# A two-network block on one core: the second network in three tiles of 1024 tokens instead of four of 768

## The chip, the core and the metric

The kernel runs on one core of one Trainium2 chip. The core has five engines with instruction streams of their own: TensorE (PE) multiplies matrices, VectorE (DVE) and ScalarE (ACT) do element-wise work, GpSimd (POOL) does slower element-wise work, SyncE (SP) issues most DMAs. Products are summed in PSUM, eight banks of 512 float32 columns on 128 partitions; everything else lives in SBUF. The metric is the device time of one launch in microseconds; lower is better.

## The reference

`x` holds 4096 tokens of 640 numbers in float32. A modulation vector scales two networks that are added to `x` one after the other. The first mixes in the frequency domain (Fourier transform along the tokens, small complex layers, inverse transform). The second is a gated feed-forward network:

```python
x = A_x
mod = (_silu(c) @ w_mod).reshape(c.shape[0], 6, 1, -1)
sa, ca, ga, sb, cb, gb = (mod[:, 0], mod[:, 1], mod[:, 2], mod[:, 3], mod[:, 4], mod[:, 5])
h = _layernorm(x, axis=-1) * (1 + ca) + sa
x = x + ga * _A_ref(h, A_w1, A_b1, A_w2, A_b2)
h = _layernorm(x, axis=-1) * (1 + cb) + sb
x = x + gb * ((_silu(h @ w_gate) * (h @ w_up)) @ w_down)
```

`w_gate` and `w_up` are 640 x 1728, `w_down` is 1728 x 640.

## The kernel before

The first network takes the first 307 us and isn't touched, apart from the last rows of it: the inverse transform of most row blocks is done while the second network runs. A *row block* is 128 tokens, and there are 32.

**Products in three parts.** Float32 products are made from a high and a low part of each operand: high by high, high by low, low by high, three products on PE. So each weight and each activation is *split*: ACT writes the high part, DVE subtracts it to get the low part.

**Tiles.** `TL` (L1142) lists the tiles of the second network as (first row block, half the number of row blocks H). Tiles 0 and 1 (`NS` = 2) have 4 row blocks, 512 tokens, and are computed plainly (`plain`, L1983). Tiles 2 to 5 have 6 row blocks, 768 tokens, in two halves of H = 3. Each of their weight pairs is a *unit of seven* (`seven`, L2104): a 2 x 2 block product by Winograd's form of Strassen's scheme, 7 block products instead of 8, with 128 H = 384 columns each, and then the fifth slice of the 640 inputs (`fifth`). In order: B11, T3, B21, fifth, T2, T4, fifth, T1, B22, fifth, fifth. A block product is 6 products on PE, a fifth 3.

**Stages of a tile.** `WG` lists 14 weight pairs: g and u (gate and up, 256 columns of the hidden 1728) for p = 0 to 5, s (the last 64 columns of both, stage 2, `rest` in tiles 2 on) and m (128 columns of both, last). `STG` orders them: g0, u0, s, g1, down 0, u1, g2, down 1, and so on to u5, m, down 5. A down stage adds the hidden columns of one p to the output of the tile's row blocks, in products of 320 columns; down 5 also adds the tail (hidden 1536 on; weights `NPR`). In tiles of `DT` (L1163: the last two) the down stage is itself a block product with seven parts per pair of row blocks (`down7`, L2265), else it is `down` (L2385).

**Places.** `bufs` (L1182) gives the number of SBUF places for each tag. R and h1: raw gate and up weights. wb: their split form. wt: the block sums T1 to T4 of a unit, in two halves (T3 and T2; T4 and T1), made once from the raw weights by `sum_w` (POOL, ACT, DVE) in tiles 0 and 1, written to DRAM (`td`) and loaded by each later tile (`load_t`, L2517). wd, wdh, wdl: raw down weights, high and low part. h0 to h7: a tile's normalised, split tokens, read back from DRAM (`hsd`) by `load_h` (L1854) in the order `HORD`; the unit uses h0, h6, h1, h3 (fifth), h5, h2, h4, h7 in this order. ho: tokens on their way to DRAM.

**Rows.** For each later tile `row_chain` (L1831) finishes the first network pair by pair of row blocks: load, gate (POOL), split, inverse transform (PE, `py`), residual and layer norm, transposes (PE, `pt`), the sums for seven block products, split, and four stores to `hsd`. `W` in `pair_steps` are these stores.

**Order.** The program order of each engine is made while the kernel is built. `slot` moves a model clock ahead with PE's products; `sweep` lets each chain of steps, in order of priority, issue what its model says is due. `until` forces a step that PE now needs. Places are taken and given back in the model through `room`. On the chip the order is fixed and semaphores hold each instruction until its operands are there; each engine's stream and SP's stream of DMA issues run strictly in order.

Of the kernel before, what the change touches and what calls it, by code (L numbers as in the profile page):

```python
# [6 lines left out]
F32 = mybir.dt.float32  # L7
# [159 lines left out]
def body(tc, x, w1, b1, w2, b2, wg, wu, wd, c, wm, k_fa, k_tb, k_tx, k_bx, k_ga, k_ge, k_id, out, dbg=None):  # L167
# [29 lines left out]
    with ExitStack() as top:  # L197
# [939 lines left out]
        with ExitStack() as ff:  # L1137
# [4 lines left out]
            TL = [(0, 2), (4, 2), (8, 3), (14, 3), (20, 3), (26, 3)]  # L1142
# [8 lines left out]
            NW = len(WG)  # L1151
            STG = []
# [10 lines left out]
            DT = (4, 5)  # L1163
# [18 lines left out]
            bufs = {"R": 2, "h1": 1, "wb": 2, "wt": 3, "wd": 1, "wdh": 2, "wdl": 2, "pc": 4, "px": 2, "gt": 2, "ho": 2,  # L1182
# [183 lines left out]
            place("wt", [P, 2, 2, 2, P], F32R, 2, "wt0_0a")  # L1366
            place("R", [P, 5, 256], F32, 2, "r0_2")
            place("h1", [P, 5, 256], F32, 1, "r0_1")
            ht0 = [fp.tile([P, 2, 512], F32R, tag=f"h{j}", bufs=1, name=f"ht0_{j}") for j in HT0]
            place("h0", [P, 4, 2, P], F32, 1, "ts0")  # L1370
            place("pc", [P, D], F32, 4, "cr0_0")
            place("px", [P, D], F32, 2, "x0_0")
            place("wd", [P, 2, D], F32, 1, "wdr0_0")
# [32 lines left out]
            prep, wld, wtl, down_w, left_l, x2_l, sums, parts, outs = [chain() for _ in range(9)]  # L1406
# [8 lines left out]
            def rtag(t, n):  # L1415
                return "h1" if t < NS and n % 3 == 1 else "R"

            def load_w(t, n):
# [3 lines left out]
                def load():  # L1422
                    r = raw[t, n] = take(tag, [P, 5, 256], F32, bufs[tag], f"r{t}_{n}")
# [7 lines left out]
                return Step("S", 2.1, load, key=("raw", t, n), use=(tag,))  # L1431


            def prep_w(t, n):
# [4 lines left out]

                def high(ks, e=slice(0, c)):  # L1440
                    if (t, n) not in wbs:
                        wbs[t, n] = take("wb", [P, 2, 5, 256], F32R, 2, f"wb{t}_{n}")
                    act.activation(wbs[t, n][:, 0, ks, e], raw[t, n][:, ks, e], AF.Copy)  # L1443

                def low(ks, e=slice(0, c)):
                    (pool if onp else dve).tensor_tensor(wbs[t, n][:, 1, ks, e], raw[t, n][:, ks, e],  # L1446
# [4 lines left out]
                if spl:  # L1451
# [3 lines left out]
                        raw[t, n][:, k2, e2], raw[t, n][:, 1:4:2, 0:P], raw[t, n][:, 0:4:2, 0:P], op=OP.subtract),  # L1455
# [64 lines left out]
            def block_loads(t, p):  # L1520
                def load(hl, s):
                    if s == 0:
                        wds.setdefault((t, p), {})
                    q = ("wdh", "wdl")[hl]
                    w = take(q, [P, 2, D], F32R, 2, f"{q}{t}_{p}_{s}").rearrange("p a (b e) -> p (a b) e", b=2)
                    n = 4 - s
                    nc.sync.dma_start(f32(w[:, 0:n]), wsd[p, :, hl, 4 * s:4 * s + n])
                    for i in range(n):
                        wds[t, p][BL[4 * s + i], hl] = w[:, i]

                if p == NPR:
                    def tail(hl, f):
                        w = wds.setdefault((t, p), {})
                        if hl:
                            w[hl, f] = take("px", [P, D], F32R, 2, f"tl{t}_{f}")
                            nc.sync.dma_start(f32(w[hl, f]), wsd[p, :, 1, 2 * f:2 * f + 2])
                        else:
                            v = take("h32", [P, 2, D], F32R, 1, f"th{t}")
                            nc.sync.dma_start(f32(v.rearrange("p a b -> p (a b)")),
                                              wsd[p, :, 0, 0:4].rearrange("p a b -> p (a b)"))  # L1540
                            w[0, 0], w[0, 1] = v[:, 0], v[:, 1]

                    d = tuple(("wst", p, x) for x in TB) + (("dend", t, 0),)
                    return [Step("S", 1.7 - 0.8 * hl, lambda hl=hl, f=f: tail(hl, f), d, ("wdb", t, p, hl, f),
                                 ("px",) if hl else ("h32",), bulk=0.8) for hl, f in ((0, 0), (1, 0), (1, 1))]

                return [Step("S", 2.1 - 0.4 * s, lambda hl=hl, s=s: load(hl, s),
                             tuple(("wst", p, x) for x in BL), ("wdb", t, p, hl, s), (("wdh", "wdl")[hl],), bulk=(3.0, 0.8, 0.8, 0.8, 0.8, 3.0)[p])
                        for s in range(2) for hl in range(2)]
# [43 lines left out]
            def prep_wd(t, p):  # L1593
# [19 lines left out]

                def high(f):
# [974 lines left out]
```

## Time and profile before

| | us |
|---|---|
| median of 3 runs (1423.55 to 1424.76) | 1424.37 |
| the profiled execution | 1426.34 |
| its span in the profile | 1424.6 |
| first network and start | 0 to 307 |
| tile 0, tile 1 (plain, 4 row blocks) | 307 to 454, 454 to 605 |
| tiles 2 and 3 (units of seven, `down`) | 605 to 821, 821 to 1036 |
| tiles 4 and 5 (units of seven, `down7`) | 1036 to 1228, 1228 to 1425 |

The profile is of one execution. Engines are PE, DVE, ACT, POOL and SP; a *line* is the line of the kernel that issued an instruction. "xN" counts instructions, "idle before, releaser" tells what ended an engine's idle time. PEclk is the granted clock of TensorE, 1.00 being full speed. Matmuls overlap in the pipeline, so that the time of one product is read from the distance of starts over a stretch, not from the duration of one.

### The profile page before, as it was taken

The page shows a single profiled execution, that of the slowest core. Times are in us where ns is not written, and L with a number is a line of the kernel's source. Part 1 is how long each engine was busy: PE and PEld are TensorE (multiplying, and loading weights), DVE is VectorE, ACT ScalarE, POOL GpSimd, SP SyncE. Part 2 cuts the span into 40 slices and gives each one's busy share as a digit, 9 for nine tenths or more (in the row PEclk, how much of TensorE's full clock was granted, in tenths as well). Part 3 has the DMA queues.
Part 4 walks back from the last instruction along what each step waited for, and adds up shares of the span by engine and source line. Part 5 has one row for each costly group of instructions (what it writes and reads, how often), then busy time and mean ns, then how long its engine had stood idle before and what let it go on. Part 6 is the DMA issues. An engine that isn't in the chain of part 4 may idle for free.

```text
span 1424.6 us, 24438 instructions
## 1 busy us (share of the span) xinstructions
PE 1392.1 (98%) x8840; PEld 1309.0 (92%) x8840; DVE 1094.9 (77%) x1983; ACT 732.9 (51%) x1495; POOL 535.2 (38%) x633
## 2 busy tenths in 40 slices
PE   6899999999999999999999999999999999999999
PEld 2699999868888888999999999999999999999998
DVE  8888898798786888578878777888657668567765
ACT  7855555555544654455455456555444345245432
POOL 5300330145453544224334434433325454145532
PEclk9999999999999999999999999999999999999999
DMA  9966677568669979997877998688886667966652
GB/s 376 327 226 207 215 246 240 193 192 262 256 208 341 311 261 301 350 326 237 280 273 256 358 348 279 236 269 280 307 311 232 215 218 239 354 223 215 207 191 85
DMA packets 183178, 372.17 MB, mean 261 GB/s; under 512 B 21360, under 2 KB 104368, under 8 KB 181392
## 3 DMA queue, kind: packets, MB, share of 16 engines
q1 hardware_dynamic: 175200, 355.12, 72.1%
q0 software_dynamic: 6272, 12.85, 2.8%
q10 hardware_dynamic: 1584, 2.62, 0.5%
q8 instruction: 70, 1.15, 0.3%
q14 instruction: 52, 0.43, 0.1%
HBM read 265.68 MB, written 104.86 MB: 260 GB/s over the span
## 4 chain that ended last, share of the span: by engine, by line
PE 64%; DVE 7%; DMA 3%; ACT 2%; issue 1%; POOL 1%; SPq 0%; DVEq 0%; ACTq 0%; POOLq 0%
PE pd L2458 14%; PE pw L2139 8%; PE pw L2141 8%; PE pw L2140 8%; PE pd_X L2320 5%; PE pd_Y L2320 3%; PE pw L2150 2%; PE pw L2152 2%; PE pw L2151 2%; PE pg L2004 2%; PE pg L2003 2%; PE pg L2005 2%; DMA cr<-s 2%; DVE wb L1446 1%; PE pd_Z L2320 1%
## 5 line engine op out<-in xcount | busy, mean ns | idle before, releaser
L2458 PE MATMUL pd<-wdh,a 128*128 128x320 f32 x1040 | 240.1, 311 | 1.3 <-DVE x L2430 1.3
L2458 PEld LDWEIGHTS pd<-wdh,a 128*128 128x128 f32 x1040 | 177.2, 189 | 1.9 <-DVE x L2430 1.6
L2458 PE MATMUL pd<-wdl,a 128*128 128x320 f32 x540 | 166.9, 310 | 0.0
L1446 DVE TENSOR_TENSOR wb<-r,wb 128x512 fp32r<-128x512 f32 (+3 forms) x154 | 154.3, 1012 | 12.2 <-ACT wb L1443 10.3
L2139 PE MATMUL pw<-h,wt 128*128 128x384 f32 x416 | 141.3, 340 | 2.2 <-ACT s_x L2158 2.2
L2141 PE MATMUL pw<-h,wt 128*128 128x384 f32 x416 | 140.4, 337 | 0.0
L2140 PE MATMUL pw<-h,wt 128*128 128x384 f32 x416 | 140.1, 337 | 0.0
L2430 DVE TENSOR_TENSOR x<-x,pd 128x320 f32<-128x320 f32 x240 | 109.8, 479 | 36.9 <-PE pd L2458 32.5
L1443 ACT ACTIVATE wb<-r 128x512 fp32r<-128x512 f32 (+3 forms) x170 | 117.4, 704 | 33.3 <-PE pw L2152 25.7
L2139 PE MATMUL pw<-h,wb 128*128 128x384 f32 x312 | 105.1, 337 | 0.9 <-DVE x L2430 0.9
L2140 PE MATMUL pw<-h,wb 128*128 128x384 f32 x312 | 104.8, 336 | 0.0
L2141 PE MATMUL pw<-h,wb 128*128 128x384 f32 x312 | 104.7, 336 | 0.0
L2005 PE MATMUL pg<-ht,wb 128*128 128x512 f32 x260 | 101.7, 391 | 1.6 <-DVE wb L1446 1.6
L2003 PE MATMUL pg<-ht,wb 128*128 128x512 f32 x260 | 102.4, 394 | 0.0
L2458 PEld LDWEIGHTS pd<-wdl,a 128*128 128x128 f32 x540 | 102.0, 189 | 0.3
L2004 PE MATMUL pg<-ht,wb 128*128 128x512 f32 x260 | 101.6, 391 | 0.0
L2158 ACT ACTIVATE s_x<-pw 128x384 f32<-128x384 f32 x52 | 25.4, 489 | 120.8 <-PE pw L2141 120.0
L2139 PEld LDWEIGHTS pw<-h,wt 128*128 128x128 f32 x416 | 78.2, 188 | 3.5 <-ACT s_x L2158 3.5
L1674 POOL TENSOR_TENSOR cr<-cr,gab 128x640 f32<-128x640 f32 x28 | 47.7, 1707 | 88.6 <-DMA cr<-s 74.0
L2140 PEld LDWEIGHTS pw<-h,wt 128*128 128x128 f32 x416 | 78.2, 188 | 0.0
L2141 PEld LDWEIGHTS pw<-h,wt 128*128 128x128 f32 x416 | 78.1, 188 | 0.0
L2294 DVE TENSOR_TENSOR x<-x,pd_X 128x320 f32<-128x320 f32 x144 | 64.5, 484 | 14.3 <-PE pd_X L2320 14.3
(345 smaller groups left out, 3872.9 us busy)
## 6 DMA issues: line engine op xcount, KB each, us to landing
wt<-td SPq DMA_DIRECT2D x104, 512.0 KB, 5.2
hs<-ho SPq DMA_DIRECT2D x52, 512.0 KB, 5.7
h<-hs SPq DMA_DIRECT2D x32, 768.0 KB, 9.0
r<-in_B_w_up_dram SPq DMA_DIRECT2D x36, 640.0 KB, 5.4
r<-in_B_w_gate_dram SPq DMA_DIRECT2D x36, 640.0 KB, 5.0
wdr<-wdd SPq DMA_DIRECT2D x25, 640.0 KB, 5.4
td<-wt SPq DMA_DIRECT2D x25, 512.0 KB, 5.5
g<-s SPq DMA_DIRECT2D x7, 1280.0 KB, 7.3
```

The lines of the kernel that those rows point to most:

```text
L1443: act.activation(wbs[t, n][:, 0, ks, e], raw[t, n][:, ks, e], AF.Copy)
L1446: (pool if onp else dve).tensor_tensor(wbs[t, n][:, 1, ks, e], raw[t, n][:, ks, e], f32(wbs[t, n][:, 0, ks, e]), op=OP.subtract)
L2003: mm(b, wh, hh, start=(kk == 0), stop=False)
L2004: mm(b, wh, hl, start=False, stop=False)
L2005: mm(b, wl, hh, start=False, stop=(kk == 4))
L2139: mm(b, w(0, kp), a[:, kp, 0], start=start and kp == 0, stop=False, skip_group_check=not start)
L2140: mm(b, w(0, kp), a[:, kp, 1], start=False, stop=False, skip_group_check=not start)
L2141: mm(b, w(1, kp), a[:, kp, 0], start=False, stop=kp == 1, skip_group_check=not start)
L2294: dve.tensor_tensor(x2, x2, q[:, :320], op=OP.add)
L2320: mm(bk[b, i][:, :320], x, y, start=new and j == 0, stop=j == len(seq) - 1, skip_group_check=not new)
L2430: dve.tensor_tensor(x2[:, e], x2[:, e], x[0][:, :320], op=OP.add)
L2458: mm(pd[g, hf][0][:, :320], l, m, start=i == 0, stop=i == len(s) - 1 and not (last and len(gs) > 1))
```

## The change

The last 24 row blocks are cut into three tiles of 8 (H = 4) instead of four of 6. Products of the units of seven have 512 columns instead of 384. Only the last tile is done with `down7`, which now goes through the row blocks of a half two at a time. As tokens and hidden activations of a tile take a third more SBUF, R, wdh and wdl have one place instead of two, wt two instead of three (one for each half). The tail's down weights go into h4 and h7 (in the last tile into R and h0), and the next tile's h4 and h7 are loaded after the last down product (`dlast`). Raw weights alternate between R and h1 in tiles 0 and 1; stage s uses ho later on. The stores of a row pair get a chain of their own (`hs_l`). The token tiles of tiles 0 and 1 lie in three places instead of five. Which unit's block sums are made in which of tiles 0 and 1 is given by two lists, unit 0 moving to tile 1 and m to tile 0. In the last down stage three row blocks go ahead of the tail instead of two. The diff, cut to its core:

```diff
-TL = [(0, 2), (4, 2), (8, 3), (14, 3), (20, 3), (26, 3)]
+TL = [(0, 2), (4, 2), (8, 4), (16, 4), (24, 4)]
...
+SUM0 = [4, 6, 8, 10, 12, 13]
+SUM1 = [n for n in range(NW) if WG[n][0] != "s" and n not in SUM0]
...
-DT = (4, 5)
+DT = (4,)
...
-bufs = {"R": 2, "h1": 1, "wb": 2, "wt": 3, "wd": 1, "wdh": 2, "wdl": 2, "pc": 4, "px": 2, "gt": 2, "ho": 2,
+bufs = {"R": 1, "h1": 1, "wb": 2, "wt": 2, "wd": 1, "wdh": 1, "wdl": 1, "pc": 4, "px": 2, "gt": 2, "ho": 2,
...
-        if turns[0] % 3 == 0:
+        if turns[0] % 2 == 0:
             return low_p.tile(shape, dt, tag=tag, name=name)
-        bufs = 2
+        bufs = 1
...
-HT0 = (3, 5, 2, 4, 7)
+HT0 = (3, 3, 5, 5, 2)
...
+xho = [fp.tile([P, D], F32, tag="ho", bufs=2, name=f"xn0_{i}") for i in (2, 3)]
+for j in (0, 6):
+    place(f"h{j}", [P, 4, 2, P], F32, 1, f"ts{j}")
...
-prep, wld, wtl, down_w, left_l, x2_l, sums, parts, outs = [chain() for _ in range(9)]
+prep, wld, wtl, down_w, left_l, x2_l, hs_l, sums, parts, outs = [chain() for _ in range(10)]
...
-    return "h1" if t < NS and n % 3 == 1 else "R"
+    return "h1" if t < NS and n % 2 else "ho" if t >= NS and WG[n][0] == "s" else "R"
...
-    return Step("S", 2.1, load, key=("raw", t, n), use=(tag,))
+    return Step("S", 2.1, load, (("hb", t, 7),) if tag == "ho" else (), ("raw", t, n), (tag,))
...
-    return None if WG[n][0] == "s" else n % NS
+    return None if WG[n][0] == "s" else 0 if n in SUM0 else 1
...
+    parts = ((0, 0, 4, "wdh"), (1, 0, 4, "wdl"), (0, 4, 7, "h32"), (1, 4, 6, "px"), (1, 6, 7, "px"))
+
+    def load(j):
+        hl, lo, hi, q = parts[j]
+        w = take(q, [P, hi - lo, 320], F32R, bufs[q], f"{q}{t}_{p}_{j}")
+        nc.sync.dma_start(f32(w), wsd[p, :, hl, lo:hi])
+        for i in range(lo, hi):
+            wds.setdefault((t, p), {})[BL[i], hl] = w[:, i - lo]
...
+        def tail(hl):
+            v = take(("R", "h0")[hl], [P, 2, D], F32R, 1, f"tl{t}_{hl}")
+            nc.sync.dma_start(f32(v.rearrange("p a b -> p (a b)")),
+                              wsd[p, :, hl, 0:4].rearrange("p a b -> p (a b)"))
+            for f in range(2):
+                wds.setdefault((t, p), {})[hl, f] = v[:, f]
...
+        d = tuple(("wst", p, x) for x in TB) + (("wb", t, NW - 1, 1),)
...
+    tags = ("h4", "h7") if p == NPR else ("wdh", "wdl")
...
-            wds[t, p] = [take(q, [P, 2, D], F32R, 2, f"{q}{t}_{p}") for q in ("wdh", "wdl")]
+            wds[t, p] = [take(tags[0], [P, 2, D], F32R, 1, f"wdh{t}_{p}")]
...
+            wds[t, p].append(take(tags[1], [P, 2, D], F32R, 1, f"wdl{t}_{p}"))
...
-    return out + [sm[0], A[0], sm[1], V[0], W[0], A[1], sm[2], V[1], W[1], sm[3], A[2], V[2], W[2], A[3], V[3], W[3]]
+    hs_l.add(W)
+    return out + [sm[0], A[0], sm[1], V[0], A[1], sm[2], V[1], sm[3], A[2], V[2], A[3], V[3]]
...
-HORD = (0, 6, 1, 5, 2, 3, 4, 7)
+HORD = (0, 6, 1, 3, 5, 2, 4, 7)
...
+        def load_k(j):
+            m = 2 if j < 2 else 1
+            b = take(f"h{HT0[2 * j]}", [P, m, 2, 2, 256], F32R, 1, f"ht{t}_{j}")
...
+                 ((("dlast", t - 1),) if j in (4, 7) else ()),
...
+    for i, (x, z, y) in enumerate((((2, 2), (0, 3), (1, 1)), ((0, 3), (1, 1), (2, 2)))):
+        if last and i:
+            x, z = (1, 1), (0, 3)
+        for j in range(2):
+            tags |= {("X", 2 * i + j): x[j], ("Z", 2 * i + j): z[j], ("Y", 2 * i + j): y[j],
+                     ("V", 2 * i + j): (0, 3)[j]}
...
+    for half in range(0, H, 2):
+        rows_ = range(half, half + 2)
+        if not last:
+            for b, ln, wn, a, hf in (("X", "A11", "B11", 0, 0), ("Z", "A12", "B21", 0, 0), ("X", "S2", "T2", 0, 1),
+                                     ("Y", "S1", "T1", 1, 1), ("X", "S3", "T3", 1, 1), ("Y", "S4", "B22", 0, 1),
+                                     ("X", "A22", "T4", 1, 0)):
+                for i in rows_:
+                    put(b, i, prod(ln, wn, i))
+                    read(b, i, a, hf, (b, wn) in (("Z", "B21"), ("Y", "B22"), ("X", "T4")))
+            continue
...
+        r = left(t, 13, 0, g)
+        return [(r, vh[:, 1, e]), (r, vl[:, 1, e]),
+                (l[0], vh[:, 0, e]), (l[0], vl[:, 0, e]), (l[1], vh[:, 0, e])]
...
+    k = 3 if last else 1
+    for gs in [tuple(range(k))] + [(g,) for g in range(k, G)]:
...
+            for key in wd_keys(t, NPR):
+                until(key)
+                wait_pe(done[key])
             for g in gs:
+                need(13, (2 * g // G,))
                 for hf in range(2):
-                    s = tail_seq(g, hf)
+                    for l, m in tail_seq(g, hf)[:2]:
+                        mm(pd[g, hf][0][:, :320], l, m, start=False, stop=False)
...
+    for tag in ("wdh", "wdl") + (("h4", "h7") if last else ()):
+        room[tag].append(x)
+    if last:
+        done["dlast", t] = x
...
-for n in (1, 2, 0):
+for n in (1, 2):
```

More of the change, by code (lines that the diff above doesn't have):

```diff
@@ L1364, in body @@
             place("ra1", [P, 512], F32R, 1, "a12l")
-            place("rb0", [P, 512], F32R, 1, "a13")
[L1366 to L1371, printed above, removed]
+            place("wt", [P, 2, 2, 2, P], F32R, 1, "wt0_0a")
+            place("R", [P, 5, 256], F32, 1, "r0_2")
+            place("wd", [P, 2, D], F32, 1, "wdr0_0")
+            place("h1", [P, 5, 256], F32, 1, "r0_1")
+            ht0 = []
+            for j in range(3):
+                b = fp.tile([P, 2, 2, 512] if j < 2 else [P, 1, 2, 512], F32R, tag=f"h{HT0[2 * j]}", bufs=1, name=f"ht0_{j}")
+                ht0 += [b[:, i] for i in range(2 if j < 2 else 1)]
+            place("pc", [P, D], F32, 4, "cr0_0")
+            place("rb0", [P, 512], F32R, 1, "a13")
             place("px", [P, D], F32, 2, "x0_0")
-            place("wd", [P, 2, D], F32, 1, "wdr0_0")
             for f in range(2):
@@ L1438, in prep_w, with raw_of @@
                 onp = t in DT and WG[n][0] == "g" and 1 < WG[n][1]
+                def raw_of(ks, e):
+                    r = raw[t, n]
+                    return r[:, 5:7, :] if t >= NS and c == P and e.start else r[:, ks, e]
                 def high(ks, e=slice(0, c)):
@@ L1520, in block_loads @@
             def block_loads(t, p):
[L1521 to L1529, printed above, removed]
@@ L1531, in block_loads @@
-                if p == NPR:
[L1532 to L1545, printed above, removed]
@@ new lines, in block_loads @@
+                if p == NPR:
+                    def tail(hl):
[5 more added lines that the diff above has]
+                    d = tuple(("wst", p, x) for x in TB) + (("wb", t, NW - 1, 1),)
+                    return [Step("S", 1.7, lambda hl=hl: tail(hl), d, ("wdb", t, p, hl), (("R", "h0")[hl],), bulk=0.8)
+                            for hl in range(2)]
@@ L1642, in wd_keys @@
                 if t in DT:
-                    return [("wdb", t, p, hl, s) for hl in range(2) for s in range(2) if p < NPR or hl or not s]
+                    return [("wdb", t, p, j) for j in range(5 if p < NPR else 2)]
                 return [("wdf", t, p, f) for f in range(2)]
@@ L2267, in down7 @@
                 last = p == NPR - 1
-                for key in wd_keys(t, p) + (wd_keys(t, NPR) if last else []):
+                for key in wd_keys(t, p):
                     until(key)
@@ new lines, in out @@
+                def out(a, i):
+                    g = H * a + i
+                    if t == NT - 1:
+                        if g < 2 * H - 1:
+                            nc.scalar.dma_start(ov[:, TL[t][0] + g, :], x_row(t, g))
+                    else:
+                        done["o", t, g] = free["V"]
+                        outs.add([Step("S", 0.85, lambda: nc.sync.dma_start(ov[:, TL[t][0] + g, :], x_row(t, g)),
+                                       (("o", t, g),), ("out", t, g), bulk=3.0, free=("gx",) * (g % H == H - 1))])
@@ L2362, in down7 @@
                         out(0, i)
-                    for i in range(H):
+                    for i in rows_:
                         fin = t == NT - 1 and i == H - 1
@@ L2373, in down7 @@
                         out(1, i)
+                if not last:
+                    for i in range(H):
+                        until(("za", t, p, i))
                 x = now[0] + 0.2
                 done["dend", t, p] = x
-                for q in ("wdh", "wdl"):
-                    room[q] += [x, x]
+                for q in ("wdh", "wdl", "h32", "px", "px"):
+                    room[q].append(x)
                 for ln in LT.values():
@@ L2446, in out @@
                                        free=("gx",) * ((g % H == H - 1) if t else 2 * (g == G - 1)))])
-                for gs in ([(0, 1)] if last else [(0,)]) + [(g,) for g in range(2 if last else 1, G)]:
+                k = 3 if last else 1
+                for gs in [tuple(range(k))] + [(g,) for g in range(k, G)]:
                     pd = {}
@@ L2475, in down @@
                 x = now[0] + 0.2
-                for q in [p] + ([NPR] if last else []):
-                    for tag in ("wdh", "wdl"):
-                        room[tag].append(x if t else max(x, 0.0))
+                for tag in ("wdh", "wdl") + (("h4", "h7") if last else ()):
+                    room[tag].append(x)
+                if last:
+                    done["dlast", t] = x
                 for tag in ("a0", "a1", "a2", "a3") + (("ra0", "ra1", "rb0", "rb1") if last else ()):
@@ L2523, in body @@
             for t in range(NT):
-                for p in (0, 1, NPR, 2, 3, 4, 5) if t in DT else range(NPR + 1):
+                for p in range(NPR + 1):
                     down_w.add(prep_wd(t, p))
```

123 lines of the change are left out of this document (54 added, 69 removed).

## The prediction

> **What bounds the kernel now.** The first view is the page's busy time by engine and its chain that ended last; the second cuts the second network into its six tiles.
>
> ```profile
> PE 1392.1 (98%) x8840; PEld 1309.0 (92%) x8840; DVE 1094.9 (77%) x1983; ACT 732.9 (51%) x1495; POOL 535.2 (38%) x633
> ...
> core 0: us, PE busy (x) PEld busy (x) DVE busy (x) ACT busy (x) POOL busy (x), PEclk, DMA share, GB/s
> 307.09:454.14 147.05, 143.47 (x770) 126.52 (x769) 121.41 (x188) 74.94 (x132) 69.16 (x80) 1.00 0.75 254
> 454.14:604.81 150.67, 149.28 (x801) 132.36 (x800) 113.72 (x197) 76.26 (x141) 60.97 (x77) 1.00 0.90 311
> 604.81:821.16 216.35, 213.37 (x1314) 212.48 (x1313) 170.95 (x296) 115.94 (x237) 82.06 (x101) 0.99 0.85 290
> 821.16:1035.82 214.66, 212.43 (x1314) 210.85 (x1313) 167.72 (x296) 115.57 (x238) 80.39 (x96) 1.00 0.82 287
> 1035.82:1228.30 192.48, 192.16 (x1172) 191.84 (x1171) 132.79 (x235) 82.50 (x170) 85.80 (x74) 1.00 0.72 254
> 1228.30:1424.60 196.30, 192.40 (x1172) 191.82 (x1170) 129.54 (x232) 79.87 (x166) 84.15 (x73) 1.00 0.57 196
> ```
>
> PE is busy 97 to 100% of every tile at a granted clock of 0.99 to 1.00, so what counts is how many products PE streams, how long each is, and what PE waits for. Its waits from 307 us to the end, by releaser (us in total, times, longest):
>
> ```profile
> PE pw L2150 <- ACT s_z L2158: 2.6, 2, 1.9
> PE pw L2139 <- ACT s_x L2158: 2.2, 4, 1.0
> PE py L1691 <- DVE chl L1681: 1.7, 4, 0.9
> PE pg L2005 <- DVE wb L1446: 1.6, 2, 1.2
> PE pd L2458 <- DVE x L2430: 1.3, 1, 1.3
> PE pw L2139 <- DVE x L2430: 0.9, 1, 0.9
> PE pt L1755 <- ACT xn L1722: 0.5, 1, 0.5
> ```
>
> Together 10.8 us of 1117. From 605 us on (the four tiles that the change recuts) the same view lists the first two, the sixth and only 0.2 of the third:
>
> ```profile
> PE py L1691 <- DVE chl L1681: 0.2, 1, 0.2
> ```
>
> That is 5.9 us. Nothing else can be won there than PE's own time and these 5.9 us; anything that makes PE wait more is lost in full.
>
> **The change, part by part.** What one product costs comes from stretches in which PE never waits:
>
> ```profile
> core 0: us, PE busy (x), PEclk, DMA share, GB/s
> 1079.12:1097.96 18.84, 18.84 (x110) 1.00 0.68 237
> 487.97:501.60 13.63, 13.63 (x63) 1.00 0.93 305
> 1247.19:1252.39 5.20, 5.20 (x31) 1.00 0.89 331
> ...
> 352.12 7.04 PE pd L2458 x48
> ```
>
> The first stretch runs from the first product of two units of seven (one weight pair each) to the first product after them: 2 x 54 = 108 products of 384 columns (7 block products of 6 and 4 x 3 for the fifth slice; the view also counts those that hang over its edges), so 18.84 / 108 = 0.1744 us. The second is one plain pair, 60 products of 512 columns: 0.2272 us. The third is the remainder stage: 30 of 384 columns, 0.1733. The fourth, from the chain, is 48 products of 320 columns: 0.1467.
>
> *Products of the units of seven.* Now 4 tiles x 13 units x 54 x 0.1744 = 489.7 us; after 3 x 13 x 54 = 2106 products x 0.2272 = 478.5. A third more columns cost only 30% more. If the 0.06 us that a unit of 384 takes above 54 x 0.1733 stays with each unit, it is 10 us instead of 11.2. I take **-11.0**.
>
> *Remainder stage.* 120 x 0.1733 = 20.8 becomes 90 x 0.2272 = 20.4: **-0.4**.
>
> *Down projection.* Only the last tile is now done with seven block products; the last two were. Per pair of row blocks seven takes 6 x 21 + 20 = 146 products, the standard way 6 x 24 + 20 = 164. Six pairs of twelve were cheap, now four are: 2 x 18 = 36 products more, x 0.1467 = **+5.3**.
>
> Rows, transposes and both plain tiles issue what they did. PE's own time: -11.0 - 0.4 + 5.3 = **-6.1 us**.
>
> By the Trainium skill's "TensorE: Matmul & The Clock Gate", section Back-to-back issue gap, a product takes N/2.4 + 2.5 ns. The 702 products that go would then give back 1.8 us, not 10 to 11. The rows above disagree: 0.1744 us is 14 ns above 384/2.4, and 0.2272 is 14 ns above 512/2.4.
>
> *Waits that go.* Four tiles share 5.9 us; with three I take 4.4, **-1.5** (bounds 0 and -3). The 4.9 us before 605 stay: the sums of unit 0 leave the crowded start of tile 0 (DVE 121 of 147 us), which helps, and single places for wdh and wdl forbid splitting them before the last down stage is over, which hurts. I take 0, bounds -3 and +4.
>
> *Single places for the block weights (wt).* A half can be loaded only after the same half's last product of the unit before. For the first half that leaves T4, T1, B22, three fifths and the next B11, 33 products = 7.5 us; for the second 39 = 8.9 us. Where a down or remainder stage lies between, it covers the load. Six borders per tile have none, so 36 loads are exposed. What a load takes, from the source view of L2520 in tiles 2 and 3, and by the page for other sizes:
>
> ```profile
> DMA to landing us min/median/max: 4.2/5.5/8.8
> DMA to landing us min/median/max: 3.6/5.9/9.0
> ...
> wt<-td SPq DMA_DIRECT2D x104, 512.0 KB, 5.2
> hs<-ho SPq DMA_DIRECT2D x52, 512.0 KB, 5.7
> h<-hs SPq DMA_DIRECT2D x32, 768.0 KB, 9.0
> g<-s SPq DMA_DIRECT2D x7, 1280.0 KB, 7.3
> ```
>
> With 0.4 us to issue, the median lands 1 to 2 us in time, the slowest about 2 us late. I take **+0.6** (0 to +5). Behind such a load on SP's queue stand raw weights, row stores and outputs, none due within a unit.
>
> The Trainium skill's "Trainium Kernel Development and Optimization", section Best Practices, says to double-buffer so that DMA overlaps compute. Here the trace shows a single place that still overlaps: half a unit lies between the last use and the next.
>
> *Places h4 and h7.* They now hold the tail weights until a tile's last down product, and their tokens for the next tile are loaded only then. T1 needs h4 after 36 products (8.2 us), B22 needs h7 after 42 (9.5 us). Each is 1 MB: alone between the 5.2 us of 512 KB and the 7.3 us of 1280 KB, in a batch above 9.0. For tiles 2 to 3 and 3 to 4 I take **+0.6** together (0 to +6); on SP's queue the next wt halves and raw loads wait behind them.
>
> *The border from tile 1 to tile 2.* Tile 2 has 8 row blocks, and the last pair must be written before its tokens can be read back. The DMA queue shows the last stores of pairs one to three, then the first loads of the old tile 2:
>
> ```profile
> 449.00 1.19 SPq L1800 DMA_DIRECT2D hs<-ho  x1
> 498.75 0.37 SPq L1800 DMA_DIRECT2D hs<-ho  x1
> 542.05 2.40 SPq L1800 DMA_DIRECT2D hs<-ho  x2
> ...
> 590.06 3.37 SPq L1867 DMA_DIRECT2D h<-hs  x5
> ...
> GB/s 376 327 226 207 215 246 240 193 192 262 256 208 341 311 261 301 350 326 237 280 273 256 358 348 279 236 269 280 307 311 232 215 218 239 354 223 215 207 191 85
> ```
>
> Pairs come every 45 to 50 us, so pair four's last store is issued at about 590 and lands 5.7 later, at 596. Tile 2 starts at 605. From 596 the queue has h6, h1, h3, h5 and h2 to load, then h4 and h7, 1.05 MB each: 3.0 us at the 350 GB/s of the busiest slices, 3.4 at the 311 of tile 1. At 350, h2 lands at 612, when it is due (30 products after the start, 611.8), h4 at 615 (due 613) and h7 at 618 (due 614.5): 3 us late. At 311 it is 6. I take **+2.5** (0 to +12), since the row stores' own chain no longer holds up a row's next steps and so brings pair four forward.
>
> *Other.* The seven-way down stage now runs two row blocks at a time. DVE reads three blocks in 1.32 us while PE writes nine products (1.32 us):
>
> ```profile
> 1073.16 1.37 DVE L2294 TENSOR_TENSOR x<-x,pd_X 128x320 f32<-128x320 f32 x3 [1.27 <-PE pd_X L2320]
> 1074.48 1.37 DVE L2294 TENSOR_TENSOR x<-x,pd_Y 128x320 f32<-128x320 f32 x3
> ...
> L2294 DVE TENSOR_TENSOR x<-x,pd_X 128x320 f32<-128x320 f32 x144 | 64.5, 484 | 14.3 <-PE pd_X L2320 14.3
> L1621 DVE TENSOR_TENSOR wdl<-wdr,wdh 128x640 fp32r<-128x640 f32 x56 | 51.8, 943 | 8.2 <-ACT wdh L1617 8.2
> ```
>
> The pace stays even. A bank comes round after 9 other products (1.3 us), where it was 15 (2.2); a read takes 0.49, so 0.7 us are spare. Counted 0; one foreign DVE instruction of 0.9 us in the way would cost 0.2 to 0.5 (ten half stages, up to +4). The raw weights' single place leaves load and split a unit of 12.3 us, and DVE, busy 171 of 216 us in tile 2, has room for the split. The block sums gain time: the seven-way tile now takes the last 13 x 12.3 + 6.8 + 584 x 0.1467 = 252 us instead of the last 389.
>
> **Sum.** -6.1 - 1.5 + 0.6 + 0.6 + 2.5 = **-3.9 us**. The profiled execution took 1426.3 us (span 1424.6 and 1.7 around it) and would take 1422.4; the median of the runs, 1424.4, is 2.0 below it, so the forecast is **1420.5**.
>
> **Rivals.**
> *A, the gain is eaten.* A third of the 36 exposed wt halves land 0.25 us late each on average (+3), h4 and h7 are 1 us late twice, the border from 1 to 2 costs 3: -7.6 + 8 gives 1424.8, within 1421.5 to 1427.2. For it: tails of 8.8 and 9.0 us in the landings, DMA busy 0.82 to 0.90. Against it: medians under 6 us.
> *B, slower.* Row pair four comes late. From a last store issued after about 595, all of tile 2's loads behind h6 slide, since SP's queue stands on that store, and PE idles one for one. A step 10 us longer than the 50 us seen (602) costs 12 us: -7.6 + 12 + 1.2 = +5.6, 1430. For it: pairs have never taken under 45 us and DMA is busy 0.90 in tile 1. Against it: a fourth pair ran in tile 1 already (the first of the old tile 3), its products at 555 and 567:
>
> ```profile
> 554.89 0.88 PE py L1691 x6
> 566.67 0.88 PE py L1691 x6
> ```
>
> *C, no new waits.* All loads arrive in time and tile 0's start gets quieter: -7.6, perhaps -10: 1414.4 to 1416.8.
> *D, the change doesn't give what it says:* a product's time goes with its columns, so longer ones save nothing. At 0.1744 x 512 / 384 = 0.2325 us, PE's units stay at 489.7 us and only the +5.3 is left: +5.3 - 1.5 + 3.7 = +7.5, 1431.9. The second stretch speaks against it: 0.2272 at 512 columns already. Chance 1%. The page on TensorE of the Trainium skill, cited above, comes near this case: by its 2.5 ns the sum would be about +5.6.
>
> **How the numbers follow.** A run of this kernel tells apart about 0.2%, 2.85 us. Forecast case (1418 to 1421.5) 36%, C (below 1418) 16%, A 30%, B 17%, D 1%. Faster is the first two, 52%; same is A, 30%; slower 18%. The range 1415 to 1429 leaves out the far end of C (about 7%) and most of B (12%).
>
> **What would show it.** In the new profile, units of seven at 0.227 us a product and 12.3 us a unit; 2552 down products where there were 2516; tile 2 starting at 605 give or take 5; PE's waits listed with releasers. Waits of L2139 or L2141 on a wt load mean A; PE idle of over 5 us just after tile 2's first products, behind h loads, means B. The forecast is wrong if a product of 512 columns in a unit takes more than 0.229 us, or if PE's waits after 307 us exceed 15 us.

## The result: slower, and the profile after

The changed kernel takes **1448.4 us** (median of 4 runs, 1447.84 to 1450.52) beside 1424.2 of the kernel before on the same chip: ratio **1.0173**, 95% interval 1.0155 to 1.0191. The forecast was 1420.5 with a range up to 1429.

First the stretches of the profile after, cut at the tiles' borders (span 1446.0), columns as before:

```profile
core 0: us, PE busy (x) PEld busy (x) DVE busy (x) ACT busy (x) POOL busy (x), PEclk, DMA share, GB/s
300.70:459.50 158.80, 152.65 (x806) 134.61 (x807) 128.57 (x203) 81.14 (x143) 75.98 (x87) 0.98 0.72 241
459.50:610.10 150.60, 150.20 (x806) 133.14 (x806) 117.60 (x197) 76.42 (x140) 55.80 (x72) 1.00 0.87 305
610.10:914.10 304.00, 288.52 (x1517) 254.62 (x1516) 221.66 (x358) 144.82 (x273) 111.20 (x131) 0.97 0.73 250
914.10:1189.20 275.10, 270.75 (x1428) 239.22 (x1428) 169.34 (x277) 111.58 (x199) 62.61 (x63) 0.99 0.60 205
1189.20:1446.00 256.80, 253.41 (x1317) 222.96 (x1316) 168.03 (x270) 96.96 (x171) 104.70 (x79) 1.00 0.47 163
```

Tile 2 is the one to look at: PE stands still for 15.5 of 304 us, and its clock is 0.97. Tile 2 of before had 3.0 us and 0.99. The products themselves are as forecast. The stretch of two units of seven, 108 products, without a wait:

```profile
1189.16:1213.86 24.70, 24.70 (x111) 20.31 (x110) 6.90 (x12) 8.90 (x16) 5.05 (x4) 1.00 0.88 314
```

24.70 / 108 = 0.2287 us. To set PE's own time apart from the rest, I counted the products from the first plain unit to the last product by their columns, each at its time without a stall (512 columns 0.2275 us, 384 0.1744, 320 0.1467, the small ones 0.11 to 0.12), and took the sum from the time that passed:

| us | PE's own | left over | of it tile 0 | tile 1 | the tiles after |
|---|---|---|---|---|---|
| before | 1105.5 | 17.9 | 6.5 | 1.8 | 5.0, 3.3, 0.6, 0.6 |
| after | 1099.7 | 47.1 | 12.7 | 0.9 | 24.8, 7.5, 1.2 |

So PE's own time went down by **5.8 us**, and what is left over, waits and stretches at half clock, went up by **29**. The waits after 300 us, by releaser, the six largest of ten rows (26.4 us in all):

```profile
engine line waited for: us in total, times, longest us
PE pw L2163 <- DMA h<-hs: 5.4, 3, 1.9
PE pw L2174 <- ACT s_z L2182: 4.7, 1, 4.7
PE py L1708 <- ACT chh L1695: 3.1, 2, 2.3
PE pw L2163 <- ACT s_x L2182: 3.1, 1, 3.1
PE py L1708 <- DVE chl L1698: 3.0, 4, 1.2
PE pw L2165 <- DVE wb L1465: 2.7, 1, 2.7
```

Few and long ones have come: PE waits for token loads (h), for ACT (s_z, s_x, chh) and for DVE (chl, wb). No load of wt is in the list. (Lines are those of the changed kernel; the gate multiplication, L1674 before, is L1691 in it.)

### One wait followed back

The 4.7 us are at 705. VectorE's timeline in front of them (start, duration, engine, line, operation):

```profile
697.31 0.68 DVE L2189 TENSOR_TENSOR s_v<-pw,s_v 128x512 f32<-128x512 f32 x1
697.91 6.20 DVE L2213 TENSOR_TENSOR a<-sg,a 128x512 fp32r<-128x512 f32 x1
704.03 0.68 DVE L1465 TENSOR_TENSOR wb<-r,wb 128x512 fp32r<-128x512 f32 x1
704.63 0.68 DVE L2213 TENSOR_TENSOR a<-sg,a 128x512 fp32r<-128x512 f32 x1
705.24 0.68 DVE L2189 TENSOR_TENSOR s_x<-pw,s_x 128x512 f32<-128x512 f32 x1
```

The same instruction, L2213, takes 6.20 us and 0.68 us. What GpSimd did meanwhile:

```profile
697.66 0.75 POOL L1793 TENSOR_TENSOR sa<-h,sa 128x256 f32<-128x256 f32 x1
698.36 1.31 POOL L2210 TENSOR_TENSOR sg<-s_v,sg 128x512 f32<-128x512 f32 x1
699.62 0.89 POOL L1578 TENSOR_TENSOR B<-B,B 128x320 f32<-128x320 f32 x1
700.45 3.10 POOL L1691 TENSOR_TENSOR cr<-cr,gab 128x640 f32<-128x640 f32 x2
```

Five instructions without a gap, 697.66 to 703.55. VectorE's instruction came in during the first and ended 0.56 us after the last. I call such a run of GpSimd instructions a *train*, and a VectorE instruction that takes over 1 us more than the shortest of its line and shape *held*. Behind it the sum s_x is late, so ACT idles, and s_z reaches PE late:

```profile
705.95 0.63 ACT L2196 ACTIVATE sg<-s_x 128x512 f32<-128x512 f32 x1 [5.01 <-DVE s_x L2189]
709.22 0.58 ACT L2182 ACTIVATE s_z<-pw 128x512 f32<-128x512 f32 x1
```
```profile
709.85 0.80 PE L2174 MATMUL pw<-h,wb 128*128 128x512 f32 x1 [4.66 <-ACT s_z L2182]
710.45 0.63 PE L2175 MATMUL pw<-h,wb 128*128 128x512 f32 x1
710.87 0.63 PE L2176 MATMUL pw<-h,wb 128*128 128x512 f32 x1
```
```profile
709.30:716.20 6.90, 6.35 (x23) 6.06 (x24) 3.82 (x8) 4.62 (x9) 0.00 (x0) 0.52 1.03 372
716.20:723.00 6.80, 6.80 (x49) 6.80 (x48) 6.34 (x14) 0.47 (x1) 0.39 (x2) 1.00 0.50 142
```

After the stall the products are 0.42 us apart instead of 0.23, and the windows view shows the granted clock at 0.52 for 6.9 us: the wait costs 4.7 us and the half clock nearly another 3. Six such stretches of 3.4 or 6.8 us lie in the profile's second network, 27 us in all; before has one, of 3.4.

Who can be held shows in the source view (count; min/median/max of one in ns), for lines of like size:

```profile
L2213 DVE TENSOR_TENSOR a<-sg,a x54: 674/691/6199, 637.9 to 1422.2; 128x512 fp32r<-128x512 f32 x54
L2189 DVE TENSOR_TENSOR s_x<-pw,s_x x39: 675/691/692, 615.2 to 1411.6; 128x512 f32<-128x512 f32 x39
L2454 DVE TENSOR_TENSOR x<-x,pd x288: 432/481/490, 327.3 to 1189.4; 128x320 f32<-128x320 f32 x144
```

L2213 reads two operands from SBUF; L2189 and L2454 read one of theirs from PSUM, and none of the 444 of these two lines was ever held (s_y, s_z and s_v have rows like that of s_x, 39 each, none above 0.69 us). The Trainium skill's "SBUF — State Buffer", section Who interferes with whom, says so: a VectorE instruction with two SBUF inputs contends with a GpSimd instruction that reads SBUF, the ports that they share are an exclusive lock, and the order of issue decides who blocks. The trace agrees on who is held. Here the 6.2 us go beyond one instruction, through all that follow without a gap. That isn't always so. At 951 VectorE got in behind the second gate of a train, while the next GpSimd instruction ran:

```profile
951.38 2.28 DVE L1465 TENSOR_TENSOR wb<-r,wb 128x768 fp32r<-128x768 f32 x1
```
```profile
949.60 3.25 POOL L1691 TENSOR_TENSOR cr<-cr,gab 128x640 f32<-128x640 f32 x2
952.81 1.58 POOL L1578 TENSOR_TENSOR B<-B,B 128x320 f32<-128x320 f32 x1
```

In the second network of this trace, 22 held instructions came while the first of two or more GpSimd instructions without a gap was running: 12 got in after that one, 9 waited for all, 1 for two of four. Eight of the nine, and none of the twelve, began behind one of the short sums of 128x256 (L1793, L1509; 0.75 us). What decides it stays open.

Held time counts as busy. DVE's 222 busy us in tile 2 contain 31 of it (17 instructions, the longest held for 5.5); in tile 2 of before it was 11.5 (5 instructions).

### The profile page after: what moved, and what is told of

It is laid out like the page before. It is cut to its first block, busy times and chain, and to the rows that moved or that the text cites. A ratio compares the mean times of both kernels' runs of the same rounds, so it can differ in the third digit from the quotient of the medians.

```text
span 1446.0 us, 22375 instructions
## 1 busy us (share of the span) xinstructions
PE 1398.8 (97%) x8144; PEld 1222.2 (85%) x8144; DVE 1059.3 (73%) x1834; ACT 694.5 (48%) x1330; POOL 481.8 (33%) x564
## 4 chain that ended last, share of the span: by engine, by line
PE 77%; DVE 8%; DMA 6%; ACT 3%; issue 3%; POOL 3%; SPq 1%; DVEq 0%; POOLq 0%; ACTq 0%
PE pd L2485 16%; PE pw L2163 8%; PE pw L2165 8%; PE pw L2164 8%; PE pc L795 5%; PE pl L727 4%; PE pd_X L2346 3%; PE pg L2028 3%; PE pg L2029 3%; PE pg L2027 3%; PE pw L2174 2%; PE pw L2176 2%; PE pw L2175 2%; PE pb L631 2%; DMA h<-hs 2%
## 5 line engine op out<-in xcount | busy, mean ns | idle before, releaser
L2485 PE MATMUL pd<-wdh,a 128*128 128x320 f32 x1220 | 280.8, 312 | 0.0
L2485 PEld LDWEIGHTS pd<-wdh,a 128*128 128x128 f32 x1220 | 209.3, 190 | 1.0
L2485 PE MATMUL pd<-wdl,a 128*128 128x320 f32 x622 | 193.5, 312 | 0.0
L2454 DVE TENSOR_TENSOR x<-x,pd 128x320 f32<-128x320 f32 x288 | 132.6, 480 | 50.3 <-PE pd L2485 48.1
L2163 PE MATMUL pw<-h,wt 128*128 128x512 f32 x312 | 125.1, 401 | 5.1 <-ACT s_x L2182 3.1
L2165 PE MATMUL pw<-h,wt 128*128 128x512 f32 x312 | 123.2, 395 | 0.0
L2164 PE MATMUL pw<-h,wt 128*128 128x512 f32 x312 | 122.8, 394 | 0.0
L2163 PE MATMUL pw<-h,wb 128*128 128x512 f32 x234 | 92.3, 395 | 3.5 <-DMA h<-hs 3.5
L2165 PE MATMUL pw<-h,wb 128*128 128x512 f32 x234 | 91.7, 392 | 2.7 <-DVE wb L1465 2.7
L2164 PE MATMUL pw<-h,wb 128*128 128x512 f32 x234 | 91.8, 392 | 0.0
L1632 ACT ACTIVATE wdh<-wdr 128x640 fp32r<-128x640 f32 x56 | 38.7, 731 | 92.1 <-PE pd L2485 83.7
L2189 DVE TENSOR_TENSOR s_z<-pw,s_z 128x512 f32<-128x512 f32 x39 | 26.9, 689 | 65.6 <-PE pw L2176 52.3
L2163 PEld LDWEIGHTS pw<-h,wt 128*128 128x128 f32 x312 | 59.0, 189 | 18.3 <-ACT s_x L2182 3.5
L2165 PEld LDWEIGHTS pw<-h,wt 128*128 128x128 f32 x312 | 59.0, 189 | 13.5
L2164 PEld LDWEIGHTS pw<-h,wt 128*128 128x128 f32 x312 | 59.3, 190 | 12.1
L2213 DVE TENSOR_TENSOR a<-sg,a 128x512 fp32r<-128x512 f32 x54 | 50.2, 935 | 25.3 <-ACT a L2212 25.0
```

The costliest lines, as they stand in the source:

```text
L2163: mm(b, w(0, kp), a[:, kp, 0], start=start and kp == 0, stop=False, skip_group_check=not start)
L2164: mm(b, w(0, kp), a[:, kp, 1], start=False, stop=False, skip_group_check=not start)
L2165: mm(b, w(1, kp), a[:, kp, 0], start=False, stop=kp == 1, skip_group_check=not start)
L2454: dve.tensor_tensor(x2[:, e], x2[:, e], x[0][:, :320], op=OP.add)
L2485: mm(pd[g, hf][0][:, :320], l, m, start=i == 0, stop=i == len(s) - 1 and not (last and len(gs) > 1))
```

## The experiments

Theory P: VectorE, held behind trains of GpSimd, is late, PE waits, and the longer waits bring a half clock. Rivals: S, the single places and loads; O, the order of the program as a whole; VectorE's own load; S0, the tail's late weights in tile 0. "Left over" is PE's time above its own, as in the table above.

### The other parts of the change, with the old tiles

```diff
-TL = [(0, 2), (4, 2), (8, 4), (16, 4), (24, 4)]
+TL = [(0, 2), (4, 2), (8, 3), (14, 3), (20, 3), (26, 3)]
...
-DT = (4,)
+DT = (4, 5)
...
-k = 3 if last else 1
+k = 2 if last else 1
```

(`down7` takes three row blocks at a time again, and its tail weights lie in h4 and h7.)

> All other parts of the change, with the old four tiles of 768 (two row blocks ahead of the tail, the seven-way down stage in threes). Theory P (long trains of GpSimd instructions hold VectorE off, TensorE then waits over 2 us and its clock drops; this comes from the new tiles' timing): 1422 to 1432 us. Rival S (single places, the late h4 and h7 and the other new places cost it): 1440 or more. If both matter, between.

1478.2 us in one run, 52 more than before. P missed, and what S expected, 1440 or more, came: with the old tiles the other parts of the change cost time of their own. Three waits for loads explain some of it, and the second of these is made by where I put the tail weights:

```profile
PE pw L2163 <- DMA h<-hs: 7.9, 6, 3.1
PE pd_Y L2345 <- DMA tl<-wsd: 7.2, 2, 6.3
PE pw L2163 <- DMA wt<-td: 6.1, 4, 2.2
```

The third is worth having: with units of 9.4 us a single place for a half of wt does make PE wait; in the changed kernel, with units of 12.4 us, no wait for wt is listed. How much of the rest the changed kernel also pays this run can't say, since its products, its order and its tail differ.

### Two row blocks ahead of the tail

```diff
-k = 3 if last else 1
+k = 2 if last else 1
```

> The changed kernel with two row blocks ahead of the tail in the last down stage, as before, instead of three. It is the base of the next run. Theory P and rival S both: 1443 to 1452 us, as the changed kernel, with tile 2 still taking about 300 us.

1443.7 us in one run, as expected. It is the base of several versions below. Left over: 40.9, of it 15.4 in tile 0, 17.0 in tile 2.

### The gate multiplication planned for VectorE

```diff
-pool.tensor_tensor(crs[r], crs[r], gab, op=OP.mult)
+(dve if r >= 4 else pool).tensor_tensor(crs[r], crs[r], gab, op=OP.mult)
...
-return ([Step("P", 1.62, gated, (k("cr"),), k("crg")),
+return ([Step(*(("V", 0.83) if r >= 4 else ("P", 1.62)), gated, (k("cr"),), k("crg")),
```

> As e2_heads, and the gate multiplication of the first network's rows (L1691, 1.57 us on GpSimd, 28 times, often two in a row) goes to VectorE (about 0.87 us). Theory P: the trains get 1.6 to 3.1 us shorter, VectorE instructions held over 1 us in tile 2 fall from 31 us to under 15, tile 2 from 304 to 280 to 290 us, the whole to 1425 to 1437. Rival S: no change beyond 3 us, or slower by VectorE's 24 us of extra work.

1427.1 us in one run, 16.6 less than the run above. Left over: 24.8, in tile 2 4.5 where 17.0 were. But `Step` is what the order is planned from, so the whole order changed too, and this run alone doesn't show the cause. What stood out was one wait in tile 0, before the tail:

```profile
PE pd L2497 <- DVE wdl L1638: 5.8, 1, 5.8
```

### The block sums of the down weights later

```diff
-(("wds", p), ("tile", 1)), k("tv", x), ("m",), bulk=1.5)
+(("wds", p), ("tile", 3)), k("tv", x), ("m",), bulk=1.5)
```

> The changed kernel with the block sums of the down weights made from tile 3 on instead of from tile 1 on; nothing else. It takes 24 GpSimd instructions of 1 us and their splits out of tiles 1 and 2. Theory P: tile 2 loses 5 to 15 us less, tile 3 a little more, the whole 1434 to 1444. Rival S: 1445 to 1451.

1484.1 us in one run: a failed experiment, and neither expectation came. The source view has the sums run until 1209 us:

```profile
L1578 POOL TENSOR_TENSOR B<-B,B x24: 856/878/1333, 960.1 to 1208.9; 128x320 f32<-128x320 f32 x24
```

The last tile began at 1188, and the list of waits shows that PE stood in it:

```profile
PE pw L2163 <- ACT s_x L2182: 26.9, 1, 26.9
```

Nor did it thin the trains: held time in tile 2 rose to 43 us, with 19.5 us left over there.

### More of it in the kernel before

A second multiplication, by one, behind each gate multiplication on GpSimd:

```diff
 pool.tensor_tensor(crs[r], crs[r], gab, op=OP.mult)
+pool.tensor_tensor(crs[r], crs[r], ones[:, 0:1].to_broadcast([P, D]), op=OP.mult)
```

> The kernel before (four tiles of 768) with a second GpSimd multiplication, by one, behind each of the 28 gate multiplications: about 1.6 us longer trains on GpSimd, which is busy 38% of the time. Theory P: VectorE instructions held over 1 us rise by more than half (now 32 us after 300 us), TensorE waits more and drops its clock at places, 1429 to 1445 us. Rival: GpSimd has room, so it costs nothing: 1423 to 1428.

1439.3 us in one run against 1425.1. The 28 added ones take 42 us of an engine that is busy 38% of the time, and 14 of them arrive at the end: left over 32.0 where 17.9 were, more in tiles 0 to 3 alone. That GpSimd has room doesn't make its work free. But held time rose only from 32 to 44 us, less than by the half that was expected, and each added one also makes its row later; the two aren't separated here.

### The gate planned for VectorE in the kernel before

The two edits of the third experiment for all rows, in the old tiling.

> The kernel before with the gate multiplication on VectorE instead of GpSimd. Theory P: its TensorE waits are only 10.8 us, so at most 2 to 6 us are won: 1418 to 1423. If VectorE is short of time, 1425 to 1432.

1445.4 us, ratio 1.0147 (1.0124 to 1.0169; ratios from here on are against before). A miss: tiles 2 and 3 have only 1.6 and 2.0 us left over (5.0 and 3.3 in before), as P had it, but the order came out anew, and the last but one tile has 15.8, with this stall and a half clock at its start (I did not follow it further):

```profile
PE pw L2139 <- ACT s_x L2158: 5.6, 2, 5.3
```

An edit that goes through the planner changes the order of everything. From here on the engine is changed at execution alone, and all other instructions of every engine keep their order.

### The tail's weights earlier, with and without the gate

In tiles 0 and 1 the weights of the tail are prepared before those of p = 5; with one place for wdh and wdl, they came behind them.

```diff
-for p in range(NPR + 1):
+for p in (0, 1, 2, 3, 4, NPR, 5) if t < NS else range(NPR + 1):
```

> e3_gate_dve, and in tiles 0 and 1 the tail's down weights are made before those of p = 5 instead of after them. In e3 TensorE waited 5.8 us for the tail's low part in tile 0 and then ran 6.8 us at half clock. Theory S0 (with one place for wdh, p = 5 can only be split after the fourth down stage, and the tail stands behind it): the wait goes, tile 0 falls from 162.4 to 152 to 155 us, the whole to 1416 to 1421. Rival: VectorE or GpSimd is late there anyway: 1424 to 1430.

1430.3 us, ratio 1.0035 (1.0023 to 1.0047): a miss. The 5.8 us wait is gone, but tile 2 has 9.3 left over instead of 4.5, in an order that was made anew.

> e2_heads (gate on GpSimd) with the tail's down weights made before those of p = 5 in tiles 0 and 1; nothing else. Theory S0: tile 0 falls from 166 to 157 to 162 us, tile 2 stays near 296, the whole 1434 to 1440. Rival: 1441 to 1446.

1428.5 us in one run. Tile 0 went from 15.4 to 9.0 left over, as expected. Tile 2 went from 17.0 to 3.1 as well, which nothing in the edit does directly: the order was made anew here too.

### The causal one: only the engine of the gate, the order unchanged

In the changed kernel, with the planner untouched, so that the 28 gate multiplications are executed on VectorE at the place that the planner's order gives them:

```diff
-pool.tensor_tensor(crs[r], crs[r], gab, op=OP.mult)
+dve.tensor_tensor(crs[r], crs[r], gab, op=OP.mult)
```

> The changed kernel with the gate multiplication executed on VectorE, every other instruction of every engine in the same order (the planner still counts it on GpSimd). So nothing else is moved. Theory P: trains shorten by 1.6 to 3.1 us, VectorE instructions held over 1 us in tile 2 fall from 31 us to under 18, tile 2 from 304 to 284 to 292 us, the whole to 1428 to 1437. Rival O (the order of the program as a whole makes the loss, not the trains): 1443 to 1452.

**1432.5 us** (6 runs), ratio 1.0048 (1.0031 to 1.0065): **16 of the 24 us come back**. The whole came as P had it and against O; tile 2 came down less than expected, to 294 us, with about 20 us held where under 18 were expected. Left over: 31.2 instead of 47.1, in tile 2 14.9 instead of 24.8, in tile 0 7.9 instead of 12.7. The stretch from above, on VectorE and on GpSimd:

```profile
694.89 3.12 DVE L2213 TENSOR_TENSOR a<-sg,a 128x512 fp32r<-128x512 f32 x1
...
703.14 0.81 DVE L1691 TENSOR_TENSOR cr<-cr,gab 128x640 f32<-128x640 f32 x1
```
```profile
694.62 0.75 POOL L1793 TENSOR_TENSOR sa<-h,sa 128x256 f32<-128x256 f32 x1
695.33 1.29 POOL L2210 TENSOR_TENSOR sg<-s_v,sg 128x512 f32<-128x512 f32 x1
696.57 0.88 POOL L1578 TENSOR_TENSOR B<-B,B 128x320 f32<-128x320 f32 x1
```

The train is the same one without its two gates, 3.06 us shorter, and the same VectorE instruction takes 3.08 us less. The wait for s_z fell from 4.7 to 1.6, and no half clock follows it. A gate is also quicker on VectorE (0.82 us against 1.6), which shortens the rows' chain; that isn't fully separated here. But PE's waits for s_z, s_x and wb, which need no gate, fell from 10.5 to 4.3 us, those for chh and chl, which do, only from 6.1 to 4.7. Nor is VectorE's own load what makes PE late: it took on 28 instructions, and PE waited less.

Of what is left over in tile 2, a good part is another thing, a wait for tokens at the border from tile 1, with half clock for 6.8 us behind it:

```profile
620.67 0.77 PE L2163 MATMUL pw<-h,wt 128*128 128x512 f32 x1 [4.30 <-DMA h<-hs]
```

### The same in the other kernels

The same one-line edit in the version with the earlier tail, and in the kernel before:

> e8_tail_only with the gate multiplication executed on VectorE, order otherwise as in e8. Theory P: 2 to 8 us less than e8, 1420 to 1427. Rival O: 1427 to 1430.

1427.2 us (10 runs), ratio 1.0016 (1.0006 to 1.0025), just over P's range and in the rival's. In this order tile 2 had only 3.1 left over to begin with; 2.4 remain.

> The kernel before with the gate multiplication executed on VectorE, order otherwise unchanged. e6, where the planner moved everything with it, took 1445. Theory P: 1416 to 1423, as VectorE is held for 32 us only and TensorE waits 10.8 us in all. Rival O: 1423 to 1430.

1426.2 us (10 runs), ratio 1.0005 (0.9995 to 1.0015): no change, as the rival had it. The kernel before paid next to nothing for its gates: PE's left-over 17.9 became 18.8.

### The rest of the trains

On top of the earlier tail with its gate on VectorE, three more kinds of GpSimd instructions were executed on VectorE, one after the other, the order unchanged: the 24 block sums of down weights, the 6 multiplications of down weights in tiles 0 and 1, the 48 sums of token blocks.

```diff
-pool.tensor_tensor(src[o], src[a], src[b], op=OP.subtract)
+dve.tensor_tensor(src[o], src[a], src[b], op=OP.subtract)
...
-pool.tensor_tensor(w, w, gbb[f].unsqueeze(1).to_broadcast([P, 2, 320]), op=OP.mult)
+dve.tensor_tensor(w, w, gbb[f].unsqueeze(1).to_broadcast([P, 2, 320]), op=OP.mult)
...
-pool.tensor_tensor(o, a, b, op=op)
+dve.tensor_tensor(o, a, b, op=op)
```

> The version that came nearest (the new tiling, two row pairs ahead of the tail, its down weights before pair 5 in tiles 0 and 1, gate multiplication executed on VectorE with every other instruction in its place; 1427.24 us), and in the same way the 24 block sums of the unit's weights (L1578, 0.96 us each on GpSimd) executed on VectorE, no other instruction moved in the list of its engine. Theory P (what holds tile 2 is VectorE held behind GpSimd): tile 2 was 283.3 us there against 275 of the tensor engine's own, with 16.0 us of VectorE held by more than 1 us each; the sums are a part of those trains, so tile 2 comes down by 2 to 5 us and the time to 1422 to 1426. Rival (VectorE itself is now the late one in tile 2, 24 sums of some 0.4 us and the gate add to it): tile 2 is not shorter, 1427 to 1432.

1426.0 us (12 runs), ratio 1.0008 (0.9998 to 1.0019). On the border between the two expectations, and in tile 2 as the rival had it: no shorter (283.1 us against 283.3). Tile 0 has 11.7 left over, as without this step (11.6), and the interval overlaps the one without it, so no gain is shown.

> The version before it (new tiling, gate and block sums of the weights executed on VectorE, same order; 1426.03 us) with the 6 multiplications of down weights by their row vector (L1625, 1.5 us each on GpSimd, in tiles 0 and 1) executed on VectorE, no other instruction moved in the list of its engine. Tile 0 is still the late one there (159.9 us against 156.1 in the kernel before), with VectorE held for 5.3 us at 427 behind a train of GpSimd that two of these multiplications open. Theory P: the hold goes or halves, tile 0 comes down by 1.5 to 4 us, time 1422 to 1425. Rival (VectorE is full in tile 0, and what it does itself takes the place of what it waited for): tile 0 the same or longer, 1426 to 1429.

1423.4 us (12 runs), ratio 0.9989 (0.9978 to 1.0001). As P had it: tile 0 has 9.8 left over instead of 11.7, and VectorE's held time there fell from 10.6 to 3.0 us.

> The run beside this one, and the 48 sums of token blocks (L1793, 0.8 us each on GpSimd in a train, spread over tiles 0 to 3) executed on VectorE too, in the same order otherwise. Theory P: tiles 0 and 2 come down by another 1 to 4 us together, since most of what is left of the trains is made of these, and VectorE does one in about 0.35 us: 1419 to 1424. Rival (VectorE's own work is now what PE waits for): no gain or slower, 1425 to 1432.

**1418.0 us** (6 runs), ratio **0.9947** (0.9932 to 0.9962): this version takes 0.5% less than before, a little less than P expected. Tile 0 has 6.4 left over, tile 2 1.3, and no VectorE instruction is held over 1 us in tiles 0 and 1. VectorE did more work in tile 2 than after the change and was busy for less, and GpSimd's 111 us there became 66. The token sums (L1793), moved last, are those behind which seven of the nine holds of a whole train began. Tile 2 of this version:

```profile
606.90:889.00 282.10, 281.98 (x1527) 250.88 (x1527) 218.57 (x412) 146.58 (x275) 65.80 (x87) 1.00 0.80 276
```

> The kernel before (four tiles of 768) with the same four kinds of instructions executed on VectorE as in the version at 1418.04 us: gate multiplication, block sums of the weights, multiplication of down weights, sums of token blocks; all other instructions in the same order. It tells whether that version's gain belongs to the new tiles or to the moves. Theory P: before loses only 17.1 us above PE's own 1096.5, and moving the gate alone gave nothing (1426.18), so at most 2 to 5 us come back: 1420 to 1425, and the new tiles are what brings the rest, since their own PE time is 5.7 us less. Rival (the moves alone make the gain): 1416 to 1419.

The control: 1420.1 us (12 runs), ratio 0.9963 (0.9953 to 0.9974). The moves alone take the old tiles down by 5 us (left over 12.3 where 17.9 were), though hardly any held time remains (1.7 us where 32 were). With the moves in both, the new tiles are 2 us ahead, 1418.0 against 1420.1, and the two intervals overlap: that the new tiles gain anything at all isn't shown.

## Why the prediction was wrong, point by point

Durations without a plus or minus are of after; changes are against before.

| step | forecast | measured |
|---|---|---|
| PE's own time | -6.1 | -5.8: right (0.2287 us a product, limit 0.229; 2552 down products) |
| tile 0's and 1's waits | 0 (-3 to +4) | tile 0 +6.2, tile 1 -0.9 |
| waits that go in the tiles after | -1.5 | +24, of it 5.4 waits for h (below): the step that failed |
| wt in single places | +0.6 | 0: no wait for wt in the profile after |
| h4, h7, and the border from tile 1 to 2 | +0.6, +2.5 | 5.4 us of waits for h, 3.8 of them at the border |
| `down7` by two | 0 | 0: the last tile has 1.2 us left over |

*The failed step* is "Waits that go", with "DVE, busy 171 of 216 us in tile 2, has room" under *Other*: -1.5 us was forecast for the tiles after 605, and 24 us (33.5 left over where 9.5 were) came. The step took a busy share for room. It looked for late transfers and counted VectorE's instructions at their usual length; the trace of before held the sign that this was wrong: in tile 2 five instructions were already held, by 11.5 us. Two of these holds, one behind the other, stand ahead of the longest wait of the prediction's list, 1.9 us for s_z, and behind that wait lies the one stretch at half clock in before's second network:

```profile
663.87 6.71 DVE L1796 TENSOR_TENSOR ho<-h,ho 128x256 fp32r<-128x256 f32 x2
671.97 0.55 DVE L2165 TENSOR_TENSOR s_x<-pw,s_x 128x384 f32<-128x384 f32 x1
...
673.50 0.56 PE L2150 MATMUL pw<-h,wb 128*128 128x384 f32 x1 [1.94 <-ACT s_z L2158]
```

In after's order such holds fell in front of s_x, s_z, chh and wb, with waits of 2.3 to 4.7 us. The criterion given in the prediction, PE's waits over 15 us after 307, was met: they were 26.

*The half clock* was in no term. Six stretches with about half the clock follow stalls; by the products in them 9.6 of the 29 us are theirs (11.2 us lost where 1.6 were). The Trainium skill's "TensorE: Matmul & The Clock Gate", section HAM oscillation, describes such a throttle with a window of 3.4 us; the stretches here are one or two times as long, 3.4 and 6.8 us. By its rule of thumb it takes idle gaps above about 3.4 us; here it came after shorter ones, as the last section shows.

*Tile 0* was bounded at +4 on account of the single places of wdh and wdl; it came out at +6.2, and mostly not for that reason. After's list has no wait for wdh or wdl, and with the gate's engine alone changed 4.8 of the 6.2 are gone. With two row blocks ahead of the tail the single places do cost: PE waits 2.3 us for the tail's wdl there, and preparing the tail's weights earlier took 6.4 out of tile 0 (left over 15.4 to 9.0), in an order that was made anew.

*Rival B*, slower, had the right sign by another mechanism: tile 2 began at 610, and PE waited 3.8 us for h there, not 12. Rivals A and D didn't come either: no wt half was late, and a product took 0.2287 us, not 0.2325.

*What is shown and what isn't.* Shown, in one fixed order: with the gate multiplications on GpSimd the changed kernel takes 16 us more than with the same ones on VectorE. The same edit gave nothing in the kernel before, which has as many of them: what counts is where they fall, not their number. Rival S holds in part: every version of the new tiles waits for h (1.8 to 7.1 us in all, 5.4 in after), and before never does. Not shown: which edit of the change made that coincidence. Each edit through the planner re-made the whole order, and tile 2's left-over ran from 3.1 to 24.8 us over versions with the same products. So the remaining 8 us can't be handed out in full to parts of the change.

## What to carry to other kernels

Before costing an edit at nothing because an engine has room, look in the source view at that engine's longest instructions beside its median: held time counts as busy and tells which work is already at the mercy of another engine. VectorE's instructions with two SBUF operands should not stand ahead of what PE waits for while GpSimd runs a train. In the changed kernel, instructions of 0.4 to 0.8 us moved to VectorE cost less than what they had held up there; in the kernel before, moving the gates gained nothing. When an order is planned, test an engine's part in it by changing the engine alone and leaving the order, since a re-planned order can move a tile by 12 us by itself.

## What was not expected of the hardware

VectorE can be held for a whole train of GpSimd instructions, 6.20 us where it needs 0.68; in other trains it got in after the first. The clock of a PE that is 97% busy can halve after one short stall. In the changed kernel's timeline lone waits of 1.60, 1.68, 1.90 and 1.92 us were not followed by it, those of 2.19, 2.72, 3.12 and 4.66 us were, and so were two in a row of 0.86 and 1.04 us and two of 2.28 and 1.24 us. That is no fixed threshold: in before a lone wait of 1.94 us was followed by it, and in the third experiment a lone one of 2.78 us wasn't. Behind the wait of 3.12 us the products are 0.43 us apart:

```profile
655.07 0.79 PE L2163 MATMUL pw<-h,wt 128*128 128x512 f32 x1 [3.12 <-ACT s_x L2182]
655.66 0.63 PE L2164 MATMUL pw<-h,wt 128*128 128x512 f32 x1
656.09 0.63 PE L2165 MATMUL pw<-h,wt 128*128 128x512 f32 x1
```
